# A DeltaNet and SwiGLU kernel: where the heads of the first diagonals lie, and the order of six small steps at its start and end

## The chip, the core and the metric

The kernel runs on one core of a Trainium2 chip. The metric is the device time of one execution in microseconds, the median of several runs.

## The reference

The inputs are q, k, v of shape (4, 8, 768, 48), beta of shape (4, 8, 768), and three weight matrices. The first half is a linear attention with the delta rule, a recurrence over 768 steps for each of the 32 pairs of batch and head:

```python
k_n = k / (norm(k) + 1e-6)
for t in range(S):
    y[:, :, t] = einsum('bhd,bhde->bhe', q[:, :, t], state)
    v_old = einsum('bhde,bhd->bhe', state, k_n[:, :, t])
    state += beta[:, :, t] * einsum('bhd,bhe->bhde', k_n[:, :, t], v[:, :, t] - v_old)
```

The heads of y are then put side by side, x has 3072 rows of 384, and the second half is a feed-forward block with d_ff = 1536:

```python
g = x @ w_gate
out = (g / (1 + exp(-g)) * (x @ w_val)) @ w_out
```

## The kernel before, in words

The sequence is cut into 12 chunks of 64 steps. Within a chunk the recurrence becomes matrix products: the Gram matrix of k with itself (below its diagonal) and with q, the inverse of a triangular matrix, and products with the state. The inverse is found by substitution in blocks of 32 (`R`). A chunk's state is carried to the next by `advance`, which also makes x for that chunk; then the feed-forward block of that chunk runs on TensorE (`gate_val`, `output`; from chunk 2 on `gate_val_fast`, `output_fast`, which save products). The attention part of the next chunks is woven in between by `point`, `fill` and the like. The weights are brought in 42 pieces (`stage`, L262, a load by SyncE; most of the first 18 wait for a piece two or three before them by way of a one-word copy on GpSimd, L261), and each is converted by two passes of ScalarE (`power_step`, L274 and L280) and three of VectorE (`convert`, L293, L301, L313).

The order on each engine is written out by hand: within `manual_schedule` an engine executes its instructions in the order in which the code issues them, and waits in place for its operands. The steps that the change touches lie at the two ends.

The start, in the order of the code from L1929 on:

- `norms(0)` and `norms(1)` square k of the first two chunks on VectorE (L385), add up (L391), and GpSimd takes the root (L395). Between the square and the sums of chunk 0 VectorE clears the last columns of `qpad[0]` (L388).
- SyncE then has q of chunk 0 to load into `qpad[0]` (`load_q(0)`), and behind it on its queue k of chunks 2 and 3, q of chunk 1, v of chunk 0, q of chunk 2 and the first weights. All loads of k, q and v go through `load_heads` (L139) or `load_v` (L185).
- `turned(c, ...)` turns k or q of a chunk on TensorE (L486) and copies it out of PSUM on ScalarE (L488, L490). `first_gram(c)` makes the Gram products of chunk c, 32 of 64x64 (L645; a product of fp32 stands in the profile as two), into two banks of PSUM, one for each parity of the head. Those of chunk 1 go to the banks that the turned k of chunk 1 is copied from.
- `first_diag(c, p)` gathers the two diagonal blocks of 32 by 32 of each head into one tile `flat`, in which the 32 heads of both chunks lie side by side and j, the column, has a stride of 32: one block by ScalarE (L654), the other added by VectorE (L656), once for each parity. `low_copies` puts the blocks below the diagonal into `l_sb` on ScalarE (L669, twelve times).
- VectorE transposes `flat` (L1951), `first_n` and `first_scale` apply norms and beta, and `first_substitution` (L702, L708) inverts both blocks of all heads at once. `first_z` and `spread_z` (L712, L725, L727) put the inverse where TensorE takes it.
- Meanwhile TensorE turns k of chunks 2 and 3 and q of chunks 0 and 1 and makes their Gram products (L502). Where it has nothing to do, `unread` (L638) has it multiply constants into a bank that nobody reads.
- `first_advance` is chunk 0's `advance`: `n_products` (L735) make N, `n_copies` (L741, L749) bring it to SBUF on ScalarE and VectorE; four rounds of products (L954) with copies and sums between (L979, L990, L1002, L1014) give u; then a product with q gives Y (L1022 on), copied at L1029 and L1031, turned for each half `bp` of the batch at L1044 and copied to x at L1045. At L1015, L1032 and L1046 stands an `unread` each.
- Between the steps of `first_advance` the code from L1991 on converts the first weights; `power_step(0)`, ScalarE's two passes over piece 0, stands behind the first step.

The end: `output_fast` of the last chunk stores two tiles `o_sb` with `store` (L1608), each by two DMAs, one for each half of the partitions, all on SyncE's queue (L1610).

Of the kernel before, what the change touches and what calls it, by code (L numbers as in the profile page):

```python
# [14 lines left out]
DP = 64  # L15
R = 32
# [4 lines left out]
def kernel(  # L21
# [25 lines left out]
    nc = tc.nc  # L47

    B, H, S, D = q.shape
    NCH = S // C  # L50
# [7 lines left out]
    HH = NB * H  # L58
# [38 lines left out]
    qpad = [const.tile([128, NB, H, DP], FP32, name=f"qpad{i}") for i in range(QB)]  # L97
# [168 lines left out]
    def power_step(n):  # L266
        if n in powers or n not in staged:
            return
        dst, _, t, f0, m = pieces[n]
        power = words(hp[10 + (n // 2 % 4 if n < N_HALF else (0, 2, 3, 1)[(n + 2) % 4])])  # L270
        power = power[:, n % 2 * m : n % 2 * m + m] if n < N_HALF else power[:, 0:m]
        powers[n] = power
        words_of = staged[n].rearrange("p (f two) -> p f two", two=2)
        nc.scalar.activation(  # L274
            dst[:, t, f0 : f0 + m],
            words_of[:, :, 1].bitcast(FP32),
            ACTF.Copy,
            scale=2.0**-112,
        )
        nc.scalar.activation(power, words_of[:, :, 0], ACTF.Copy, scale=2.0**-29)  # L280
# [100 lines left out]
    def norms(c):  # L381

        ksq = work.tile([128, NB, H, D], FP32, name="ksq", tag="r", bufs=2)
        x = knp[c][:, :, :, 0:D]
        nc.vector.tensor_tensor(out=ksq, in0=x, in1=x, op=ALU.mult)  # L385
        n = n_t[0][:, c].rearrange("p (par bp j) -> p par bp j", par=2, bp=NB)
        if c == 0:
            nc.vector.memset(qpad[0][:, :, :, D - 1 : DP], 0.0)  # L388
        ksq_v = ksq.rearrange("p bp (j par) d -> p par bp j d", par=2)
        for par in range(2):  # L390
            nc.vector.tensor_reduce(  # L391
                out=n[:, par], in_=ksq_v[:, par], axis=mybir.AxisListType.X, op=ALU.add
            )
        n = n_t[0][:, c]
        nc.gpsimd.tensor_tensor(out=n, in0=n, in1=half[:, 0:HH], op=ALU.pow)  # L395
# [58 lines left out]
    def banks(name, tag):  # L454

        if type(tag) is int:
            return [ps_ffn([128, 512], name, tag + i) for i in range(2)]
        p = ps_pair(name, tag)
        return [p[:, 0], p[:, 1]]
# [142 lines left out]
    first_of, l_sb, n_sb = {}, {}, {}  # L602
# [7 lines left out]
    def first_tiles():  # L610
        a = work.tile([128, C * 2 * HH], FP32, name="a_sb")
        for c in range(2):
            l_sb[c] = a[:, R * R * c : R * R * (c + 1)].rearrange(
                "p (h k) -> p h k", k=C
            )
        first_of["flat"] = new_mb().rearrange("p k i -> p (k i)")
        first_of["diag"] = first_of["flat"].rearrange("p (j h) -> p h j", j=R)
        first_of["zb"] = places["z1"].bitcast(FP32)[:, 4 * H_ - 1056 : 4 * H_]
        first_of["mb"] = places["wo"].bitcast(FP32)[:, 2 * H_ : 2 * H_ + 1056]
        nc.vector.memset(first_of["zb"], 0.0)  # L620
        for c in range(2):
            nc.vector.memset(l_sb[c][:, :, 48:C], 0.0)
        for x, rows in enumerate((slice(16, C), slice(R, C), slice(48, C), slice(0, R))):
            nc.vector.tensor_reduce(
                out=m_two[:, x],
                in_=ident.rearrange("p (b n) -> p b n", b=2)[:, :, rows],
                axis=mybir.AxisListType.X,
                op=ALU.add,
            )
        nc.vector.tensor_tensor(  # L630
            out=m_rows, in0=m_two[:, :, 0], in1=m_two[:, :, 1], op=ALU.add
        )
        nc.vector.tensor_scalar_mul(m_low, m_rows[:, 0:3], -1.0)

    def unread(count, p, m=512):

        for _ in range(count):
            nc.tensor.matmul(p[0:R, 0:m], half, half[:, 0:1].to_broadcast([128, m]))  # L638

    def first_gram(c, tag):  # L640

        p_v = [p.rearrange("p (x h i) -> p x h i", x=2, i=R) for p in banks("p_g", tag)]
        for bp, j, par, b, _ in every():
            k_v = kt[c][half_of(par), bp, j, b].rearrange("p (x i) -> p x i", x=2)
            nc.tensor.matmul(  # L645
                p_v[par][half_of(b), :, NJ * bp + j], kt[c][half_of(par), bp, j, b], k_v
            )
        return p_v

    def first_diag(c, p):  # L650
        to = first_of["diag"][:, HH * c : HH * c + HH]
        to = to.rearrange("p (par h) j -> p par h j", par=2)
        for par in range(2):
            nc.scalar.mul(to[:, par], p[par][:, 0], m_rows[:, 3:4])  # L654
        for par in range(2):
            nc.vector.scalar_tensor_tensor(  # L656
                out=to[:, par],
                in0=p[par][:, 1],
                scalar=m_rows[:, 1:2],
                in1=to[:, par],  # L660
                op0=ALU.mult,
                op1=ALU.add,
            )
# [278 lines left out]
    def first_advance():  # L942
# [5 lines left out]
        to = nc.vector.tensor_copy  # L948
# [57 lines left out]
        for bp in range(NB):  # L1006
# [5 lines left out]
                lambda par, b, j: t[there(par, b), 1 - par, bp, j],  # L1012
            )
            plus(uu[:, :, bp], t[:, 1:3, bp], pairs[bp])  # L1014
        unread(1, banks("p_t", 0)[1], 256)  # L1015
        spread_z(1, 0, nc.vector)
        held_loads[26] = lambda: load_v(2)
        yield
# [2 lines left out]
        for bp, copy in enumerate((nc.scalar.copy, nc.vector.tensor_copy)):  # L1021
# [7 lines left out]
            copy(y[:, bp, :, 0], pairs[bp][:, 0])  # L1029
            for b in range(2):  # L1030
                copy(y[half_of(b), bp, :, 1], pairs[bp][half_of(1 - b), 1])  # L1031
        unread(1, banks("p_t", 0)[1], 256)  # L1032
        yield
        y_f = y.rearrange("p bp j par d -> p bp (j par d)")
        xts[0] = x_first
# [5 lines left out]
        for bp, copy in enumerate((nc.scalar.copy, nc.vector.tensor_copy)):  # L1041
            for k in range(KT):
                at = slice(k * 128, (k + 1) * 128)
                nc.tensor.transpose(p_f[bp][:, k], y_f[:, bp, at], ident)  # L1044
            copy(x_v[:, :, bp], p_f[bp])  # L1045
        unread(1, banks("p_t", 0)[1], 256)  # L1046
        spread_z(1, 1, nc.scalar)
        yield
# [558 lines left out]

    def store(c, bp, o_sb):  # L1608
        for b in range(2):
            nc.sync.dma_start(  # L1610
                out=out_v[NB * b + bp, c * C : (c + 1) * C],
                in_=o_sb[half_of(b)],
            )
# [172 lines left out]
    def step(kind, fn, *args):  # L1786
        key = (kind, args or (1,))
        if key not in gens:
            gens[key] = [fn(*args), 0]
        if next(gens[key][0], None) != MORE:  # L1790
            gens[key][1] += 1
# [128 lines left out]
    with tc.manual_schedule(  # L1920
# [8 lines left out]
        new_n(0)  # L1929
        load_beta()  # L1930
        first_tiles()
        norms(0)
        norms(1)
        load_q(0)
# [5 lines left out]
        unread(3, ps_pair("p_t", "px")[:, 0])  # L1940
        turned(0, False, 0)
        p_g = [first_gram(0, "px")]
        first_diag(0, p_g[0])
        turned(1, False, 2)
        p_g.append(first_gram(1, 2))
        first_diag(1, p_g[1])
        spread_beta(copy_a)
# [41 lines left out]
        new_nt(0, spare_of_q, state_flat[:, LEAD : LEAD + 512])  # L1989
        new_nt(1, zb_1.rearrange("p k i -> p (k i)"), spare_of_q[:, 0:512])  # L1990
        gens["advance", (0,)] = [first_advance(), 0]  # L1991
        step("advance", advance, 0)
        power_step(0)
        step("advance", advance, 0)
        converts_first(0)
        power_step(2)
# [110 lines left out]
```

## Time and profile before

| | us |
|---|---|
| median of 3 runs | 663.73 |
| lowest and highest | 663.14, 665.0 |
| the profiled execution | 662.01 |
| its span, first to last instruction | 660.3 |
| TensorE busy in the span | 647.3 |
| VectorE, ScalarE, GpSimd busy | 476.7, 281.5, 198.5 |

The span is what the profile can see; the execution's own time is 1.7 us longer. The mean granted clock of TensorE is 0.997 of full speed. In the rows of a timeline the first two numbers are the start in microseconds from the span's start and the duration; merged instructions have their count behind an x; in brackets stands the idle time of the engine ahead of the row and what ended it. PE is TensorE, PEld its weight loads, ACT ScalarE, DVE VectorE, POOL GpSimd, and SPq SyncE's queue. In a row of a view by stages stand the stretch and its length, each engine's busy time with its count, TensorE's granted clock, the DMA engines' mean share and GB/s.

### The profile page before, as it was taken

To read this page: it belongs to the slowest core of one execution; us is meant where nothing else is said; L and a number is where in the kernel's file an instruction comes from. 1 tells how busy PE (TensorE), PEld (TensorE's weight loads), DVE (VectorE), ACT (ScalarE), POOL (GpSimd) and SP (SyncE) were. 2 spreads that over 40 slices of the span, in tenths; PEclk is the share of its full clock that TensorE was granted. 3 is DMA by queue.
4 is the path that set the end of the run, shared out by engine and by line. 5 is a ranking of instruction groups with operands and counts; after the bars stand their busy time and mean duration, and the time that the engine had idled before them with its cause. 6 is when DMAs were issued, how large, how long until landed. Compare 5 with 4: busy or idle time off the path is not lost.

```text
span 660.3 us, 24914 instructions
## 1 busy us (share of the span) xinstructions
PE 647.3 (98%) x10856; PEld 595.8 (90%) x10856; DVE 476.7 (72%) x991; ACT 281.5 (43%) x626; POOL 198.5 (30%) x310
## 2 busy tenths in 40 slices
PE   8899999999999999999999999999999999999997
PEld 4568888767999999999999999999999999999997
DVE  6879799999688767758667758677758655655562
ACT  5788867124336433434433433532333433334230
POOL 7130041023894032880031881031881000000000
PEclk9999999999999999999999999999999999999999
DMA  9668762005742551373454274363363442222321
GB/s 135 142 173 272 205 164 101 1 14 99 195 81 69 103 117 51 93 140 84 104 127 88 61 164 92 85 135 98 72 136 85 100 105 66 62 94 66 87 66 25
DMA packets 147438, 68.57 MB, mean 104 GB/s; under 512 B 123456, under 2 KB 126560, under 8 KB 147328
## 3 DMA queue, kind: packets, MB, share of 16 engines
q1 hardware_dynamic: 144992, 66.48, 42.6%
q8 instruction: 85, 1.39, 0.8%
q10 hardware_dynamic: 2080, 0.39, 0.4%
q0 software_dynamic: 256, 0.10, 0.1%
q14 instruction: 25, 0.20, 0.1%
HBM read 59.08 MB, written 7.86 MB: 101 GB/s over the span
## 4 chain that ended last, share of the span: by engine, by line
PE 85%; DVE 6%; DMA 4%; SPq 2%; issue 1%; ACT 1%; POOL 0%; DVEq 0%; ACTq 0%; POOLq 0%
PE ffn L1407 40%; PE ffn L1683 21%; PE ffn L1564 8%; DMA h_f<-in_moe_w_val_dram 3%; PE ffn L1593 2%; PE p_px L1169 2%; SPq L139 2%; PE p_py L502 1%; DVE x_t L587 1%; DVE zb L593 1%; PE p_py L1071 1%; PE p_px L1152 1%; PE p_py L1088 1%; PE p_px L502 1%; PE p_px L923 1%
## 5 line engine op out<-in xcount | busy, mean ns | idle before, releaser
L1407 PE MATMUL ffn<-x_t,w_gv 128*128 128x128 f32 x800 | 108.7, 279 | 0.8 <-DVE p_sb L1633 0.7
L1407 PEld LDWEIGHTS ffn<-x_t,w_gv 128*128 128x128 f32 x800 | 97.4, 192 | 3.9 <-DVE p_sb L1633 1.8
L1441 ACT ACTIVATE sil<-ffn 128x256 f32<-128x256 f32 x100 | 36.4, 383 | 115.4 <-PE ffn L1407 109.3
L1407 PE MATMUL ffn<-x_ffn,w_gv 128*128 128x128 f32 x640 | 84.6, 275 | 0.0
L1683 PE MATMUL ffn<-wo_sb,h_f 128*128 128x192 f32 x480 | 83.9, 328 | 0.0
L1683 PEld LDWEIGHTS ffn<-wo_sb,h_f 128*128 128x128 f32 x480 | 77.9, 190 | 0.6
L1407 PEld LDWEIGHTS ffn<-x_ffn,w_gv 128*128 128x128 f32 x640 | 78.0, 192 | 0.3
L822 POOL TENSOR_TENSOR n_b<-mb,half 128x32 f32<-128x32 f32 x5 | 27.6, 5520 | 159.2 <-DVE mb L556 159.2
L587 POOL TENSOR_TENSOR h_f<-zb,mb 128x31 f32<-128x31 f32 (+15 forms) x124 | 69.3, 559 | 19.2 <-PE p_py L800 6.0
L593 POOL TENSOR_TENSOR zb<-zb,h_f 128x31 f32<-128x31 f32 (+15 forms) x124 | 70.6, 569 | 9.7
L1407 PE MATMUL ffn<-x_t,h_f 128*128 128x128 f32 x472 | 64.7, 280 | 0.0
L1407 PEld LDWEIGHTS ffn<-x_t,h_f 128*128 128x128 f32 x472 | 57.3, 192 | 1.6 <-DVE ffn L1633 0.5
L1442 DVE TENSOR_TENSOR h_f<-sil,ffn 128x256 f32<-128x256 f32 x100 | 39.3, 418 | 23.8 <-ACT sil L1441 23.8
L1103 ACT COPY x_ffn<-p_py 32x256 f32<-32x256 f32 (+3 forms) x108 | 39.3, 364 | 29.0 <-PE p_py L1088 27.3
L1633 DVE TENSOR_TENSOR ffn<-p_sb,ffn 128x512 f32<-128x512 f32 x40 | 27.8, 695 | 25.8 <-PE ffn L1407 25.1
L1636 DVE TENSOR_TENSOR ffn<-ffn,p_sb 128x512 f32<-128x512 f32 x40 | 27.5, 691 | 19.9 <-PE ffn L1407 19.1
L1683 PE MATMUL ffn<-last_k,h_f 128*128 128x192 f32 x200 | 36.0, 327 | 0.0
L1636 DVE TENSOR_TENSOR o_sb<-o_sb,ffn 128x192 f32<-128x192 f32 x50 | 17.5, 350 | 24.2 <-PE ffn L1683 23.7
L1564 PE MATMUL ffn<-x_t,w_gv 128*128 128x256 f32 x144 | 33.9, 385 | 0.2 <-DVE x_t L1045 0.2
L1683 PEld LDWEIGHTS ffn<-last_k,h_f 128*128 128x128 f32 x200 | 32.9, 190 | 0.1
L1564 PE MATMUL ffn<-x_ffn,w_gv 128*128 128x256 f32 x144 | 31.9, 380 | 0.0
L1407 PE MATMUL ffn<-x_ffn,h_f 128*128 128x128 f32 x232 | 30.9, 276 | 0.0
(330 smaller groups left out, 1172.7 us busy)
## 6 DMA issues: line engine op xcount, KB each, us to landing
h_f<-w_s SPq DMA_DIRECT2D x81, 256.0 KB, 2.8
more_w<-w_s SPq DMA_DIRECT2D x27, 256.0 KB, 2.8
vin<-in_v_dram SPq DMA_DIRECT2D x48, 96.0 KB, 3.5
out_dram<-o_sb SPq DMA_DIRECT2D x48, 96.0 KB, 2.2
kn<-in_k_dram SPq DMA_DIRECT2D x20, 192.0 KB, 4.7
zt<-in_moe_w_out_dram SPq DMA_DIRECT2D x10, 384.0 KB, 4.3
qpad<-in_q_dram SPq DMA_DIRECT2D x36, 64.0 KB, 3.0
w_s<-h_f SPq DMA_DIRECT2D x7, 256.0 KB, 2.8
```

Source lines behind the costliest of these rows:

```text
L139: dmas[b % len(dmas)].dma_start(out=t[64 * b : 64 * b + 64, :, :, 0:D].rearrange("p bp h d -> p (bp h) d"), in_=halves(x, c, b).rearrange( ...
L587: engine.tensor_tensor(out=t_v, in0=zb[:, 0 : j + 1, j : j + 1].to_broadcast([128, j + 1, m]), in1=mb[:, j : j + 1, j + 1 : R].to_broadcas ...
L593: engine.tensor_tensor(out=zb[:, 0 : j + 1, j + 1 : R], in0=zb[:, 0 : j + 1, j + 1 : R], in1=t_v, op=ALU.add,)
L822: nc.gpsimd.tensor_tensor(out=n, in0=mb.rearrange("p j i -> p (j i)")[:, 0 : R * R : R + 1], in1=half, op=ALU.pow,)
L1103: nc.scalar.copy(x_all[at % 128 : at % 128 + rows, at // 128].rearrange("p (bp b i) -> p bp b i", bp=NB, b=2), p[64 * half + lo : 64 * hal ...
L1407: nc.tensor.matmul(p[:, u], w(u), moving, start=start and u == 0, stop=True, skip_group_check=True,)
L1441: nc.scalar.activation(silu_of, p[:, 0:2], ACTF.Silu)
L1442: nc.vector.tensor_tensor(out=h_of(c, PAIRS[r][e % 3], e // 3), in0=silu_of, in1=p[:, 2:4], op=ALU.mult)
L1564: nc.tensor.matmul(ps[name][:, i], w_sb[:, t, (f + i) * 128 : (f + i + 1) * 128], xts[c][:, t], start=(t == 0 and i == 0), stop=(t == KT - 1),
L1633: nc.vector.tensor_tensor(out=out, in0=a, in1=b, op=ALU.subtract)
L1636: nc.vector.tensor_tensor(out=out, in0=a, in1=b, op=ALU.add)
L1683: nc.tensor.matmul(p[x, part], a(f - f % 2)[:, f % 2], b(f), start=not begun and f == 0, stop=f == FH - 1, skip_group_check=True,)
```

## The change

Six edits:

1. The clearing of `qpad[0]`'s last columns goes from within `norms(0)` to the line ahead of it.
2. In `first_gram` the heads become the innermost dimension of a bank: a product's 64 columns are written at a step of 8 words. `first_diag` then goes over the same order in both places, eight heads side by side, where it read 32 neighbours and wrote them at a stride of 32 words. `low_copies` is not changed, but its reads from PSUM now have a step of 8 words.
3. `first_diag(0)` takes a function to call between its two passes on ScalarE; it is called with the turning of k of chunk 1, whose copies so stand between those passes. TensorE's order stays.
4. `power_step(0)` goes ahead of the first step of `first_advance`, so ScalarE's passes over piece 0 stand ahead of its copy of N.
5. Of the `unread` products in `first_advance`, those ahead of Y's products and behind them are dropped, and one is added between the turnings of the two halves of Y.
6. In the last chunk one of the two DMAs of each `store` is issued by ScalarE in place of SyncE.

```diff
-        if c == 0:
-            nc.vector.memset(qpad[0][:, :, :, D - 1 : DP], 0.0)
...
-        first_of["diag"] = first_of["flat"].rearrange("p (j h) -> p h j", j=R)
...
-        p_v = [p.rearrange("p (x h i) -> p x h i", x=2, i=R) for p in banks("p_g", tag)]
+        p_v = [p.rearrange("p (x i h) -> p x h i", x=2, i=R) for p in banks("p_g", tag)]
...
-    def first_diag(c, p):
-        to = first_of["diag"][:, HH * c : HH * c + HH]
-        to = to.rearrange("p (par h) j -> p par h j", par=2)
+    def first_diag(c, p, between=None):
+        to = first_of["flat"].rearrange("p (j c par h) -> p c par j h", c=2, par=2, j=R)
+        to = to[:, c]
+        p = [p_h.rearrange("p x h j -> p x j h") for p_h in p]
         for par in range(2):
             nc.scalar.mul(to[:, par], p[par][:, 0], m_rows[:, 3:4])
+            if between and par == 0:
+                between()
...
             plus(uu[:, :, bp], t[:, 1:3, bp], pairs[bp])
-        unread(1, banks("p_t", 0)[1], 256)
         spread_z(1, 0, nc.vector)
...
                 copy(y[half_of(b), bp, :, 1], pairs[bp][half_of(1 - b), 1])
-        unread(1, banks("p_t", 0)[1], 256)
         yield
...
             copy(x_v[:, :, bp], p_f[bp])
+            if bp == 0:
+                unread(1, banks("p_t", 0)[1], 256)
         unread(1, banks("p_t", 0)[1], 256)
...
-            nc.sync.dma_start(
+            queue = nc.scalar if c == NCH - 1 and b == bp else nc.sync
+            queue.dma_start(
...
         first_tiles()
+        nc.vector.memset(qpad[0][:, :, :, D - 1 : DP], 0.0)
         norms(0)
...
-        first_diag(0, p_g[0])
-        turned(1, False, 2)
+        first_diag(0, p_g[0], lambda: turned(1, False, 2))
...
+        power_step(0)
         step("advance", advance, 0)
-        power_step(0)
         step("advance", advance, 0)
```

## The prediction

> **What bounds the kernel now.** First the page: its first line says whose time it is.
>
> ```profile
> PE 647.3 (98%) x10856; PEld 595.8 (90%) x10856; DVE 476.7 (72%) x991; ACT 281.5 (43%) x626; POOL 198.5 (30%) x310
> ...
> q8 instruction: 85, 1.39, 0.8%
> ```
>
> TensorE idles 13 of 660.3 us. In a kernel so full, an edit pays where TensorE still waits: the first 48 us and the last 4, where all six edits lie. The span is 660.3 us and the profiled execution 662.01, so 1.7 us lie around the span; the median of the three runs, 663.73, is 1.7 above that execution. The sum is made against 662.01.
>
> Next the chain of waits over the first 70 us (start, us, what):
>
> ```profile
> 0.82 4.71 DMA kn<-in_k_dram
> ...
> 6.60 0.30 DVE qpad L388
> ...
> 6.91 0.60 SPq L139
> ...
> 21.94 1.39 SPq L262
> ...
> 42.00 4.12 DMA h_f<-in_moe_w_val_dram
> ...
> 48.30 1.15 PE p_px L1152 x64
> ```
>
> From 48.30 on it is nearly all TensorE. Ahead of that it is SyncE's row of loads, begun behind the memset of L388, and then weights landing. Beside this runs a second chain of nearly equal length, read from the timelines of single engines: k turned, Gram products, diagonals, substitution, N, x. ScalarE and VectorE there:
>
> ```profile
> 8.52 1.17 ACT L654 ACTIVATE mb<-p_px,m_rows 128x256 f32<-128x256 f32 x2 [0.82 <-issue]
> 9.49 1.11 ACT L488 COPY kt<-ffn 128x512 f32<-128x512 f32 x2
> 11.85 1.17 ACT L654 ACTIVATE mb<-ffn,m_rows 128x256 f32<-128x256 f32 x2 [1.25 <-PE ffn L645]
> ...
> 14.25 1.67 ACT L669 ACTIVATE a_sb<-p_px,m_low 128x128 f32<-128x128 f32 x6
> ...
> 17.25 1.18 ACT L490 COPY kt<-p_py 128x512 f32<-128x512 f32 x2
> ...
> 27.27 0.75 ACT L725 ACTIVATE zt<-mb,m_rows 128x256 f32<-128x256 f32 x1 [2.58 <-DVE mb L712]
> ...
> 33.43 0.48 ACT L990 COPY uu<-p_px 128x384 f32<-128x384 f32 x1 [0.98 <-PE p_px L954]
> ...
> 46.14 0.44 ACT L274 ACTIVATE w_gv<-h_f 128x256 f32<-128x256 f32 x1 [0.49 <-DMA h_f<-in_moe_w_val_dram]
> ...
> 47.47 0.79 ACT L1050 COPY state<-p_px 128x768 f32<-128x768 f32 x1
> ...
> 12.59 1.32 DVE L656 SCALAR_TENSOR_TENSOR mb<-ffn,m_rows,mb 128x256 f32<-128x256 f32 x2 [1.08 <-ACT mb L654]
> 13.95 1.25 DVE L1951 STREAM_TRANSPOSE wo_sb<-mb 128x1024 f32<-128x1024 f32 x1
> ...
> 7.90 5.81 POOL L395 TENSOR_TENSOR n_t<-n_t,half 128x16 f32<-128x16 f32 x2 [0.35 <-DVE n_t L391]
> ```
>
> and TensorE:
>
> ```profile
> 10.65 1.16 PE L645 MATMUL ffn<-kt 64*64 64x64 f32 x62 [0.16 <-ACT kt L488]
> ...
> 23.79 3.63 PE L638 MATMUL ffn<-half 128*32 128x512 f32 x8
> ...
> 28.08 1.16 PE L735 MATMUL ffn<-zt,a_sb 64*64 64x64 f32 x64 [0.66 <-ACT zt L725]
> ...
> 32.63 0.73 PE L954 MATMUL p_px<-v,qpad 64*64 64x48 f32 x22 [1.62 <-issue]
> ...
> 36.63 0.51 PE L954 MATMUL p_px<-x_t,qpad 64*64 64x48 f32 x21 [0.32 <-issue]
> ...
> 39.45 0.62 PE L638 MATMUL ffn<-half 128*32 128x256 f32 x2
> ...
> 40.13 1.17 PE L1044 MATMUL ffn<-ident,y 128*128 128x128 f32 x6
> 40.76 0.31 PEld L1044 LDWEIGHTS ffn<-ident,y 128*128 128x128 f32 x3 [0.32 <-DVE y L1031]
> ...
> 41.24 0.62 PE L638 MATMUL ffn<-half 128*32 128x256 f32 x2
> ```
>
> The two stalls marked "issue" wait for no data. Between 32.63 and 36.63 lie 24 + 32 + 64 + 8 = 128 products. The page has 85 instruction packets of 1.39 MB, 16 KB each; 21,712 products and weight loads in 1.39 MB are 64 bytes apiece, so a packet holds 128 product-and-load pairs. I read the stalls as TensorE waiting for its next block of code, asked for when the block before the last is left: about 4.0 us from one block's entry to the next (32.63 to 36.63), 4.5 the time before (28.08 to 32.63). If so, N's start at 28.08 sets 32.63 and 36.63, and whatever ScalarE does between is covered.
>
> **The change part by part.**
>
> *Memset of qpad ahead of norms(0).* The first load of q (and all of SyncE's row behind it) waits for it:
>
> ```profile
> 3.31 0.17 DVE L633 TENSOR_SCALAR m_low<-m_rows 128x3 f32<-128x3 f32 x1
> ...
> SPq L139 <- DVE qpad L388: 4.4, 1, 4.4
> ...
> 7.00:8.00 1.00, 0.76 (x48) 0.73 (x50) 0.75 (x2) 0.71 (x2) 0.65 (x3) 1.00 0.33 46
> ...
> 14.00:15.00 1.00, 0.67 (x2) 0.00 (x0) 1.00 (x1) 1.00 (x4) 0.00 (x0) 1.00 1.53 160
> ```
>
> Second row: SyncE idles 4.4 us for L388. VectorE is free from 3.5 us (first row), so q is issued near 3.8 instead of 6.91. The transfers cannot gain all 3.1 us: those of k fill the engines first. What goes is the hole behind them, in which 46 GB/s flow (third row, last column) against the 160 of a full microsecond (fourth): 0.7 us, and with its edges about 0.95. Bounds 0.7 and 3.1; I take 1.1, near the hole, because the stretch around 14 us is full in any case. SyncE's DMAs keep their order, so k(2), v and all weights come earlier by this. The early q shares the engines with k(1)'s end; only norms(1) waits for k(1) alone, and it delays L656 of chunk 1 only when it comes more than about 0.9 us later.
>
> *Diagonals side by side.* The four L654 and four L656 lose their stride of 32 words in SBUF. Rows by form:
>
> ```profile
> L654 ACT ACTIVATE mb<-ffn,m_rows 128x256 f32<-128x256 f32 x2 | 1.2, 694 | 1.2 <-PE ffn L645 1.2
> L656 DVE SCALAR_TENSOR_TENSOR mb<-ffn,m_rows,mb 128x256 f32<-128x256 f32 x2 | 1.3, 706 | 1.1 <-ACT mb L654 1.1
> L274 ACT ACTIVATE w_gv<-h_f 128x256 f32<-128x256 f32 x2 | 0.9, 434 | 0.0
> L301 DVE SCALAR_TENSOR_TENSOR w_gv<-w_gv,h_f 128x256 uint32<-128x256 uint32 x10 | 4.0, 420 | 0.2
> ```
>
> Equal sizes without the stride (last two rows) take 434 and 420 ns, against 694 and 706. From chunk 1's Gram to the transpose stand one L654 and two L656: 2.10 us (11.85 to 13.95) becomes some 1.3. Gain 0.8 on VectorE's chain. In exchange 64 Gram products write PSUM at a step of 8 words and twelve L669 read it so. No row has a PSUM step. Bounds (no gain: nothing there has a stride to lose): L669 as now (1.67 us for six), or as much more as L725, which reads SBUF at a stride, has over L274 (0.75 - 0.43 us for 256 elements, 0.16 for 128): 0 to 1.9 us for twelve; a Gram 1.16 us as now, or double. I take nothing: a product of 512 columns takes 0.45 us (3.63 / 8 at 23.79), a pace at which a step need not show; both ends stay.
>
> *Turned k(1) between the two ScalarE passes.* The copies (L488) start when their four transposes are done, about 9.0 (the first L654, now 0.43, is over by then), not 9.49: the second Gram, which waits for both copies since it writes their banks (row at 10.65), ends 0.48 earlier. ScalarE's second L654 comes after them, at about 10.1, and its reader on VectorE is still through before chunk 1's.
>
> So VectorE's chain comes 0.48 + 0.8 = 1.28 earlier at L1951, which then ends at 13.9. The norms follow it, and GpSimd's two powers end at 13.7 (7.90 + 5.81; 0.2 sooner without the memset), so they still do not come last. The substitution keeps its length, and L725 at 27.27 becomes 26.0. ScalarE's row (L669, k(2), k(3), q copies) and TensorE's unread products come 0.48 earlier: they end at 26.95 instead of 27.43 (23.79 + 3.63). N starts at the later of 26.95 and 26.75 (26.0 and L725's 0.75): 26.95 instead of 28.08. **Gain 1.1 us**, now set by TensorE's own unread products.
>
> *Piece 0's passes ahead of N's copies.* 0.75 us of ScalarE (L274, L280) move from 31.70 to about 27.7. Queued behind them are N's copy (0.25 later than the shift) and v's copies; the products after them stop at the code stall in any case. At the old place ScalarE waited 0.98 (row at 33.43). So nothing either way: the stall covers it; with the cover gone, 0.3 lost and up to 0.5 gained.
>
> *Unread products.* The one before Y and the one after it go: TensorE then waits where it multiplied (about 0.7 and 0.6 us). The new one, two passes (0.62 in all, 0.4 of it passing), sits ahead of the second turnings, which now begin at 40.76 and would wait for it until about 40.9: 0.1 on x, less than the unread product ahead of the first gate that x waits beside. I take nothing; bounds -0.1 and 0.2.
>
> *State and weights.* The state copy at 47.47 follows ScalarE's passes, which waited 0.49 for a weight. With both chains 1.1 earlier, L1152 starts at about 47.2. Everything behind keeps its distances. Sum so far: -1.1.
>
> *Last stores.*
>
> ```profile
> 656.16 0.35 DVE L1636 TENSOR_TENSOR o_sb<-o_sb,ffn 128x192 f32<-128x192 f32 x1 [1.60 <-PE ffn L1683]
> 656.60 1.11 SPq L1610 DMA_DIRECT2D out_dram<-o_sb  x2
> ```
>
> Two issues of 0.55 in a row become one on each queue; ScalarE has nothing left. At most 0.55 goes, less if the two transfers then slow each other: I take 0.45.
>
> Total: -1.1 - 0.45 = **-1.55**: 660.5 for an execution like the profiled one, 662.2 against the median.
>
> The Trainium skill speaks against the diagonals: PSUM — Partial Sum Buffer, Specifications, has PSUM lines of 8 bytes and says that any non-contiguous pattern slows matmuls significantly. No row here shows it; by that rule the steps cost, and the time is that of the third rival below.
>
> **The rivals.**
>
> *More than that.* TensorE's code stall of 1.62 us shrinks because the block's fetch meets a quieter queue, or SyncE's 3.1 us count more fully. For it: with 4.0 instead of 4.5 us per block, 0.5; with the stall gone, another 0.5. Then -1.1 - 1.0 - 0.45 = -2.55: **661.2**. Against it: weight loads are in flight in both kernels.
>
> *Only the tail.* The weights land as late as now (42.00 in the chain, and 46.14 on ScalarE), since each load waits for the one two before it, and the state copy stays at 47.47; the change then does not do what it says at the start. For it: the wait of 0.49. Against: their first issue, at 21.94, stands in SyncE's row. -0.45: **663.3**.
>
> *Slower: steps in PSUM.* Place: the 64 Gram products and twelve L669. Grams double: second Gram's end 1.2 later instead of 0.48 earlier; L669 adds 1.9; TensorE's unread products end at 27.43 + 3.1 = 30.5, N starts 2.4 later; less the tail 0.45: +2.0, **665.7**. It decides from 0.48 + 0.65 (N's present wait behind the unread products) + 0.45 = 1.6 us on that row of ScalarE. For it: every strided SBUF row above is slower by 0.26 to 0.32. Against: fp32 products pass slowly.
>
> *The clock.* After the stall of 1.62 the granted clock fell by half:
>
> ```profile
> 33.00:34.00 1.00, 1.00 (x48) 1.00 (x44) 0.97 (x2) 0.48 (x1) 0.98 (x2) 0.50 0.21 78
> ```
>
> With two unread products gone, gaps of 0.7 and 0.6 us could call a second such stretch, near 40 us: some 0.7 us of its products, so -0.85, **662.9**. The microseconds around 14.67 to 15.78 idled 1.1 without it (clock 1.00 in the row at 14), so I hold it unlikely. The Trainium skill, TensorE: Matmul & The Clock Gate, "HAM oscillation", wants idle of a window of about 3.4 us before the clock falls; the trace shows it after less, so that sentence is no comfort here.
>
> **How the numbers follow.** Forecast 662.2: 42 in 100, spread about 0.8 either way by what the clock does. More, 661.2: 25. Only the tail, or the clock: 18 together. Steps: 15, of which half is one of the two costs alone (about 664) and half the whole, 665.7 and above. 0.3% (2.0 us) is about what a measurement of this kernel can tell from no change: faster is below 661.74, slower above 665.72. Faster: nearly all of the second and 4 in 10 of the first, 0.42. Slower: 0.09. Within: 0.49. The range from 660.4 to 665.0 leaves out about 1 in 10 at either end.
>
> **What would show it.** Right: SyncE's q issue near 3.8; L654 and L656 near 0.43 in mean; L735 at about 27.0; L1152 at about 47.2; stores landing 0.45 earlier behind the last VectorE add. Wrong: L645 or L669 longer than now; L735 later than 28.08; the 128-pair stalls not moving with L735; a second 0.50 in the clock; or a time that moves without L1152.

## The result and the profile after

The kernel after takes 662.66 us in the median of 20 executions (659.75 to 665.33), the kernel before 664.94 in 20 executions beside it (663.04 to 669.79). The ratio is 0.9967 with a 95% interval from 0.9954 to 0.9981: 2.2 us faster, between 1.3 and 3.1. The forecast was 1.55 us.

The profiled execution of the kernel after took 662.8 us, with a span of 661.1; that of before, on which the prediction's sum stands, took 662.01, which is below the lowest of the 20 executions measured beside the kernel after. So the two traces can't be subtracted as wholes; stage by stage they can. The page's first line, after:

```profile
PE 647.7 (98%) x10854; PEld 595.2 (90%) x10854; DVE 476.4 (72%) x991; ACT 281.0 (43%) x626; POOL 198.6 (30%) x310
```

TensorE has two passes less (one fp32 product of `unread`) and idles 13.4 of 661.1 us, against 13.0 of 660.3. Next VectorE's timeline of the kernel after at the start:

```profile
3.48 0.28 DVE L1933 MEMSET qpad<- 128x272 f32 x1
...
10.56 0.88 DVE L656 SCALAR_TENSOR_TENSOR mb<-p_px,m_rows,mb 128x256 f32<-128x256 f32 x2 [0.21 <-ACT mb L652]
11.91 0.88 DVE L656 SCALAR_TENSOR_TENSOR mb<-ffn,m_rows,mb 128x256 f32<-128x256 f32 x2 [0.47 <-ACT mb L652]
12.82 1.25 DVE L1952 STREAM_TRANSPOSE wo_sb<-mb 128x1024 f32<-128x1024 f32 x1
```

The clearing is done at 3.8, the pairs of L656 take 0.88 us instead of 1.32, and the transpose begins at 12.82 instead of 13.95. ScalarE (L652 is the former L654):

```profile
8.53 0.47 ACT L652 ACTIVATE mb<-p_px,m_rows 128x256 f32<-128x256 f32 x1 [0.82 <-PE p_px L642]
9.08 1.07 ACT L486 COPY kt<-ffn 128x512 f32<-128x512 f32 x2
10.04 0.49 ACT L652 ACTIVATE mb<-p_px,m_rows 128x256 f32<-128x256 f32 x1
11.41 0.84 ACT L652 ACTIVATE mb<-ffn,m_rows 128x256 f32<-128x256 f32 x2 [0.88 <-PE ffn L642]
13.31 0.32 ACT L430 COPY beta_b<-p_py 128x192 f32<-128x192 f32 x1 [1.07 <-PE p_py L423]
13.90 1.07 ACT L486 COPY qt<-ffn 128x512 f32<-128x512 f32 x2 [0.27 <-PE ffn L484]
14.86 1.67 ACT L669 ACTIVATE a_sb<-p_px,m_low 128x128 f32<-128x128 f32 x6
16.36 1.71 ACT L669 ACTIVATE a_sb<-ffn,m_low 128x128 f32<-128x128 f32 x6
...
26.15 0.75 ACT L725 ACTIVATE zt<-mb,m_rows 128x256 f32<-128x256 f32 x1 [0.85 <-DVE mb L712]
...
45.35 0.44 ACT L274 ACTIVATE w_gv<-wo_sb 128x256 f32<-128x256 f32 x1 [0.88 <-DMA wo_sb<-in_moe_w_gate_dram]
...
46.03 0.78 ACT L1050 COPY state<-p_px 128x768 f32<-128x768 f32 x1
```

Up to 12 us the row is as forecast. Then ScalarE waits 1.07 us for L423, the spreading of beta on TensorE, and the six L669, forecast 0.48 earlier than 14.25, stand at 14.86. TensorE:

```profile
10.21 1.16 PE L642 MATMUL ffn<-kt 64*64 64x64 f32 x62 [0.16 <-ACT kt L486]
...
12.43 0.85 PE L423 MATMUL p_py<-wo_sb,ident 16*32 16x192 f32 x8 [0.29 <-DMA wo_sb<-in_beta_dram]
...
24.40 3.63 PE L635 MATMUL ffn<-half 128*32 128x512 f32 x8
27.96 1.16 PE L735 MATMUL ffn<-zt,a_sb 64*64 64x64 f32 x64
...
30.24 0.76 PE L954 MATMUL p_px<-v,qpad 64*64 64x48 f32 x29 [0.19 <-ACT v L979]
...
34.49 0.51 PE L954 MATMUL p_px<-x_t,qpad 64*64 64x48 f32 x21 [0.62 <-issue]
...
45.16 0.35 PE L735 MATMUL ffn<-zt,a_sb 64*64 64x64 f32 x9 [0.62 <-issue]
...
46.93 1.15 PE L1152 MATMUL p_px<-state,kt 48*64 48x48 f32 x64
...
56.55 0.72 PE L1196 MATMUL p_px<-v,zb 64*64 64x48 f32 x33 [1.58 <-issue]
```

N starts at 27.96, only 0.12 us earlier than before. L1152 starts at 46.93 instead of 48.30, since the "issue" stall of 1.62 us in the n-times-v products is not there (30.24). But a stall of 1.58 us now stands at 56.55, where this execution loses all of that again. What holds the start is seen in the chain of waits of the kernel after, and in the issues of beta's loads in the first 14 us (KB each, median us from issue to landing), first before, then after:

```profile
7.03 5.26 DMA wo_sb<-in_beta_dram
12.43 0.85 PE p_py L423 x8
...
14.97 3.10 ACT a_sb L669 x12
...
24.47 2.90 PE ffn L635 x7
```

```profile
wo_sb<-in_beta_dram POOLq DMA_DIRECT2D x4, 20.0 KB, 2.9
wo_sb<-in_beta_dram POOLq DMA_DIRECT2D x4, 4.0 KB, 3.2
```

```profile
wo_sb<-in_beta_dram POOLq DMA_DIRECT2D x4, 20.0 KB, 5.1
wo_sb<-in_beta_dram POOLq DMA_DIRECT2D x4, 4.0 KB, 5.6
```

The early load of q shares the DMA engines with beta's eight small loads, which GpSimd issues from 2.7 to 7.5 us in both kernels. In these two executions they take 2.2 to 2.4 us longer, TensorE waits for them at L423, and ScalarE and TensorE's row to N behind it.

The end, after:

```profile
657.19 0.35 DVE L1637 TENSOR_TENSOR o_sb<-o_sb,ffn 128x192 f32<-128x192 f32 x1 [1.59 <-PE ffn L1684]
657.62 0.53 ACTq L1611 DMA_DIRECT2D out_dram<-o_sb  x1
657.64 0.47 SPq L1611 DMA_DIRECT2D out_dram<-o_sb  x1
```

The last tile's two stores are issued side by side. From the end of the last add (657.54) to the end of the span (661.06) it is 3.52 us; before it was 3.79.

### The profile page after: what moved, and what is told of

Same layout as the page of the kernel before. It is cut to its first block, busy times and chain, and to the rows that moved or that the text cites. A ratio compares the mean times of both kernels' runs of the same rounds, so it can differ in the third digit from the quotient of the medians.

```text
span 661.1 us, 24911 instructions
## 1 busy us (share of the span) xinstructions
PE 647.7 (98%) x10854; PEld 595.2 (90%) x10854; DVE 476.4 (72%) x991; ACT 281.0 (43%) x626; POOL 198.6 (30%) x310
## 4 chain that ended last, share of the span: by engine, by line
PE 82%; DVE 8%; ACT 4%; DMA 3%; issue 2%; POOL 1%; DVEq 0%; ACTq 0%; SPq 0%; POOLq 0%
PE ffn L1407 40%; PE ffn L1684 21%; PE ffn L1564 4%; PE ffn L1593 2%; DMA zt<-in_moe_w_out_dram 2%; PE p_px L1169 2%; DVE x_t L585 1%; DVE zb L591 1%; PE p_px L500 1%; PE p_py L500 1%; PE p_py L1071 1%; PE p_px L923 1%; PE p_py L1088 1%; PE p_px L1152 1%; DMA wo_sb<-in_beta_dram 1%
## 5 line engine op out<-in xcount | busy, mean ns | idle before, releaser
L822 POOL TENSOR_TENSOR n_b<-mb,half 128x32 f32<-128x32 f32 x5 | 27.6, 5520 | 160.9 <-DVE mb L554 160.9
```

Source lines behind the costliest of these rows:

```text
L822: nc.gpsimd.tensor_tensor(out=n, in0=mb.rearrange("p j i -> p (j i)")[:, 0 : R * R : R + 1], in1=half, op=ALU.pow,)
```

## The experiments

The theory behind the first runs (A): the gain comes from VectorE's chain, the diagonals; the early clearing costs through beta; the stalls marked "issue" are TensorE's waits for code. The first rival: the gain comes from SyncE's earlier row. All medians stand beside the kernel before on the same chip; "us against before" is the ratio's interval times its median there (664.2 to 664.8). Each run's profile is of one execution; those of e7 and e8 are the longest of their twelve. A pair number counts TensorE's product-and-load pairs from the start of the program; by the prediction's reading a block of code holds 128 of them, and a border is where one block ends.

| run | edits of the change | median | us against before |
|---|---|---|---|
| e1 | 1 | 663.93 | -0.9 (-1.9 to +0.1) |
| e2 | 2, 3 | 661.25 | -3.3 (-4.6 to -2.1) |
| e3 | 6 | 663.71 | -0.3 (-1.6 to +1.0) |
| e4 | all but 1 | 662.17 | -2.1 (-3.3 to -0.9) |
| e5 | 4, 5 | 663.37 | -1.1 (-2.4 to +0.1) |
| e6 | all, 24 more pairs ahead of N | 665.12 | +1.1 (-0.5 to +2.7) |
| e7 | all, beta spread later | 662.29 | -2.2 (-3.5 to -0.8) |
| e8 | all, both of these | 664.24 | -0.4 (-1.7 to +0.9) |
| e9 | 2, 3, 6 | 661.75 | -2.9 (-3.8 to -1.9) |
| e10 | 2, 3, 6, two more unread | 662.02 | -2.9 (-4.1 to -1.8) |
| e11 | 1, 2, 3, 6, beta later, two more unread | 662.08 | -2.4 (-3.5 to -1.3) |
| e12 | all, beta later, two more unread | 662.42 | -2.0 (-3.5 to -0.5) |

**e1, the early clearing alone.**

```diff
-        if c == 0:
-            nc.vector.memset(qpad[0][:, :, :, D - 1 : DP], 0.0)
...
+        nc.vector.memset(qpad[0][:, :, :, D - 1 : DP], 0.0)
         norms(0)
```

> The kernel before with edit 1 alone (the clearing of qpad[0] ahead of norms(0)). Theory A (beta's collision): q's early transfer takes DMA time from beta's eight small loads on GpSimd's queue, which land near 12.3 us instead of about 10; TensorE waits for beta at L425 until about 12.4, ScalarE's row from L488 (copies of the turned q) on is 0.4 to 0.7 us later than before, N's start (first L735 row) is at 28.1 to 28.7 us, not earlier, and the median lies within 0.5 us of before, although the first weight pieces land 0.8 us earlier. Theory B (my forecast's step): SyncE's whole row comes 1.1 us earlier, ScalarE's row does not come later, and L1152 starts some 0.5 to 1 us earlier: about -0.8 us.

Beta's loads took 5.2 and 5.6 us, N started at 28.75 us, L1152 at 49.91, and the median is 0.9 us below before, with an interval that just includes nothing. A is right on beta's loads, but not on the median, which fits B; B's earlier L1152 isn't in this trace, that of the second longest of twelve executions. On N the run decides nothing. The first diagonal pass came 0.68 us late by itself (9.20), so that beta was there at L423, and N starts as far behind that pass as before: 19.55 us, against 19.56.

**e2, the diagonals alone.**

```diff
...
-        p_v = [p.rearrange("p (x h i) -> p x h i", x=2, i=R) for p in banks("p_g", tag)]
+        p_v = [p.rearrange("p (x i h) -> p x h i", x=2, i=R) for p in banks("p_g", tag)]
...
-        first_diag(0, p_g[0])
-        turned(1, False, 2)
+        first_diag(0, p_g[0], lambda: turned(1, False, 2))
```

> The kernel before with edits 2 and 3 alone (heads side by side in the diagonals, the copies of k(1) between the two passes). Theory A: VectorE's chain is 1.1 to 1.3 us earlier (L725 on ScalarE at about 26.1 instead of 27.27), and, as beta is not delayed here, ScalarE's row and TensorE's unread products are 0.4 to 0.5 us earlier too, so N starts at 26.9 to 27.1 instead of 28.08. The weights stay where they were, so that L1152 gains less than N: -0.3 to -1.0 us in the median. Theory B (the gain of the whole change comes from SyncE's row): N starts earlier but the median stays within 0.3 us of before. Theory C (a step in PSUM costs): L645 or L669 longer than the 1.16 and 1.67 us of before by 0.2 or more.

The largest gain of any single part, more than A expected: 3.3 us. The Gram took 1.15 us and six L669 1.68: C (a step in PSUM) falls. N started at 27.45, 0.5 later than expected, because this execution's first diagonal pass was 0.5 us late (9.03). Behind that pass N comes 18.42 us later, 1.14 less than before.

**e3, the two queues alone.**

```diff
+            queue = nc.scalar if c == NCH - 1 and b == bp else nc.sync
-            nc.sync.dma_start(
+            queue.dma_start(
```

> The kernel before with edit 6 alone (one of each two last stores issued by ScalarE). Theory A (issue is serial on one queue): the last transfer is issued 0.55 us earlier, the span behind the last VectorE add shrinks by 0.2 to 0.55 us, median -0.2 to -0.55. Theory B (most of the 2.3 us of the whole change comes from the tail): -1 us or more.

From the last add's end to the span's end: 3.53 us here, 3.52 in the kernel after, 3.55 in e4 and 3.53 in e9; without the edit 3.79 before, 3.78 in e1, 3.88 in e2. So 0.2 to 0.4 us in each pair of traces, which a median can't resolve. B falls.

**e4, everything but the early clearing.**

```diff
+        if c == 0:
+            nc.vector.memset(qpad[0][:, :, :, D - 1 : DP], 0.0)
...
-        nc.vector.memset(qpad[0][:, :, :, D - 1 : DP], 0.0)
         norms(0)
```

> The kernel after with edit 1 undone (the clearing back within norms(0)). Theory A: without q's early transfer beta lands near 10 us as in the kernel before, ScalarE's row is about 1 us earlier than in the kernel after (first L669 row at 13.8 instead of 14.86), N starts at 26.9 to 27.1 instead of 27.96; but the weights land 0.8 to 1.5 us later than in the kernel after, so L1152 starts at about 47.3 to 47.8. Median -1.0 to -2.0 us against before, about that of the kernel after. Theory B (SyncE's row carries the gain): L1152 back near 48.3 and the median within 0.7 us of before.

Beta's loads took 3.7 and 4.4 us, the first L669 stood at 14.19, N at 27.30 and L1152 at 47.91. The median is that of the kernel after (-2.1 against -2.2): no gain from the early clearing shows in this company, with intervals of about 1 us either way, and B falls. N's start 0.66 us earlier does not show in the median either.

**e5, the pass over piece 0 and the unread products alone.**

```diff
+        power_step(0)
         step("advance", advance, 0)
-        power_step(0)
         step("advance", advance, 0)
...
-        unread(1, banks("p_t", 0)[1], 256)
         spread_z(1, 0, nc.vector)
...
-        unread(1, banks("p_t", 0)[1], 256)
         yield
         y_f = y.rearrange("p bp j par d -> p bp (j par d)")
...
             copy(x_v[:, :, bp], p_f[bp])
+            if bp == 0:
+                unread(1, banks("p_t", 0)[1], 256)
```

> The kernel before with edits 4 and 5 alone (ScalarE's passes over piece 0 ahead of N's copies; the unread products of first_advance). Theory A: nothing at the start moves, N starts at 28.1 us as before, what is saved or lost between N and Y lies beside TensorE's waits for code; median within 0.6 us of before. Theory B: the gaps left by the dropped unread products lower the granted clock more often than before (mean clock of the executions below before's by 0.002 or more), +0.7 to +1.7 us. Theory C: these two edits carry part of the gain, -0.7 us or more.

N started at 28.36 us and L1152 at 49.68. The median is 1.1 us below before with an interval from -2.4 to +0.1: not told apart from nothing. A loss of more than 0.1 us is excluded; whether they gain is not settled, for A's and C's medians both lie in the interval. B falls: the mean clock is 0.9962, and 0.9959 before.

**e6, 24 more pairs of code ahead of N.**

```diff
-        unread(4, banks("p_t", 2)[0])
+        unread(16, banks("p_t", 2)[0], 128)
```

> The kernel after, in which the four unread products of 512 columns ahead of N are sixteen of 128 columns: the same columns, 24 more product-and-load pairs ahead of N, nothing else. Theory A (TensorE's issue stalls are waits for a block of 128 pairs of code): the stalls stay at the pairs with the numbers 600, 728, 984 and 1240, which are now products that stand 24 earlier in the kernel's order, and the border at pair 472 is crossed among the unread products, near 26 us, instead of just behind N's start at 28; so the next blocks come up to 2 us earlier and the stalls between N and Y together are 0.5 to 1.5 us shorter; median 0.3 to 1.5 us below the kernel after, -2.5 to -3.7 against before. Theory B (the stalls wait for data or for another engine): they stay at the same products of the kernel's order, whose pair numbers are then 624, 752, 1008; the median stays at that of the kernel after.

TensorE's timeline in e6:

```profile
23.76 2.07 PE L635 MATMUL ffn<-half 128*32 128x128 f32 x17
27.07 1.82 PE L635 MATMUL ffn<-half 128*32 128x128 f32 x15 [1.24 <-issue]
28.82 1.16 PE L735 MATMUL ffn<-zt,a_sb 64*64 64x64 f32 x64
...
31.06 0.39 PE L954 MATMUL p_py<-vin,zt 64*64 64x48 f32 x13 [0.39 <-issue]
```

On the place A is right: the stall that stood 8 products deep in the n-times-v products stands 24 earlier in the order, at pair 600 again, and pair 728 has its stall again (0.67 us, at 34.79). On the time: a stall of 1.24 us opens in the middle of the unread row, at pair 473. The 16 KB that landed last ahead of it were on their way from 24.21 to 25.79; in the kernel after they were in at 25.26, and their border was reached only at N's start. N starts 0.86 later than in the kernel after. And yet this is not where the run loses: counted product by product, TensorE is 0.8 us ahead of the kernel after from 60 us on, as A has it, because the stall of 1.58 at 56.55 is gone. It falls behind at 534 us, where a second new stall opens:

```profile
535.89 0.82 PE L1407 MATMUL ffn<-x_t,w_gv 128*128 128x128 f32 x5 [1.64 <-issue]
```

It stands three products behind the 128 small ones of L905, and 16 KB of code landed 1.37 us ahead of its end, as at the stalls near the start. Among the other runs only e8 has it. So the 24 pairs moved the borders of the whole program, and a late one came to lie badly. The median is 2.5 us above the kernel after, and A is wrong on it. This trace is of one of the six shorter executions (662.66 to 664.30); the six longer ones (665.94 to 668.15, mean clock 0.986 to 0.994) left none, so why they are longer stays open.

**e7, beta spread behind q's turning.**

```diff
-        spread_beta(copy_a)
         turned(0, True, 0)
+        spread_beta(copy_a)
```

> The kernel after with spread_beta behind the turning of q of chunk 0 instead of ahead of it. Theory A (beta's late landing holds TensorE and, through it, ScalarE's row): the copies of the turned q start at about 12.6 instead of 13.90, the first L669 at 13.6 to 14.2 instead of 14.86, N starts at 26.9 to 27.2 instead of 27.96, then set by L725 on ScalarE (26.15 + 0.75); 0.3 to 1.0 us below the kernel after. Theory B (N's start is held by something else on ScalarE or TensorE): N's start stays at 27.7 or later and the median within 0.3 us of the kernel after.

ScalarE and TensorE in e7:

```profile
13.86 1.66 ACT L669 ACTIVATE a_sb<-p_px,m_low 128x128 f32<-128x128 f32 x6
```

```profile
27.15 1.16 PE L735 MATMUL ffn<-zt,a_sb 64*64 64x64 f32 x64
...
32.20 0.51 PE L954 MATMUL p_px<-v,qpad 64*64 64x48 f32 x21 [2.12 <-issue]
```

Beta's loads still took 5.2 and 5.6 us, but nothing waited for them: the first L669 came 1.0 us and N 0.81 us earlier than in the kernel after, as A has it. The median did not follow (-2.2 both). The last row shows a reason in this execution, the longest of twelve: the earlier N ran into a longer wait for code.

**e8, both.** The two diffs of e6 and e7 together.

> The kernel after with both of the two other edits of this call: spread_beta behind q's turning, and sixteen unread products of 128 columns in place of four of 512. Theory A: both gains, N's start at about 27 and the border at pair 472 crossed near 25; 0.8 to 2.3 us below the kernel after, -3 to -4.5 against before. Theory B: once the next block of code sets the pace between N and Y, an earlier start of N is covered, and the two together bring no more than the shift alone.

2.0 us above e7, as e6 is 2.5 above the kernel after: the cost of the shifted code borders repeats, and both theories of this run were too hopeful. The late stall is at the same product:

```profile
538.58 1.27 PE L1407 MATMUL ffn<-x_t,w_gv 128*128 128x128 f32 x5 [1.69 <-issue]
```

Behind it, from 538.79, lie 3.41 us at half clock. Up to 527 us this trace is 1.4 us ahead of e7's, from 540 us on 2.2 behind.

**e9, the diagonals and the tail.** The diffs of e2 and e3 together.

> The kernel before with edits 2, 3 and 6 alone (diagonals side by side, the copies of k(1) between, the two queues of the last stores): the change without the early clearing, the early pass over piece 0 and the moves of unread products. Theory A (the diagonals carry the gain, the early clearing gives part of it back through beta): N starts at 27.2 to 27.6 us, at the same granted clock 2.4 to 3.4 us below before, so -2.3 to -3.7 in the median. Theory B (the low median of the run with the diagonals alone was chance): -0.7 to -1.6, no more than the whole change.

ScalarE, then TensorE, in e9:

```profile
13.77 1.67 ACT L671 ACTIVATE a_sb<-p_px,m_low 128x128 f32<-128x128 f32 x6
```

```profile
23.32 3.63 PE L637 MATMUL ffn<-half 128*32 128x512 f32 x8
26.91 1.16 PE L737 MATMUL ffn<-zt,a_sb 64*64 64x64 f32 x64
...
31.02 0.51 PE L956 MATMUL p_px<-v,qpad 64*64 64x48 f32 x21 [1.19 <-issue]
```

This is the start that the prediction worked out: L669 0.48 earlier than before, N at 26.91 (26.95 forecast), still set by the unread row. The median is 2.9 us below before: A, though N comes earlier than the 27.2 to 27.6 that A gave.

Ahead of e10 the price that its expectation puts on the clock: of the 25 executions of before beside e1 to e4, five with a mean clock of 0.997 took 663.27 us in mean, three with 0.991 665.42 (but five with 1.000 took 663.84). Over all kernels to e9 it is some 3.5 us for 0.01 of clock, or 0.9 for 3.41 us at half, which are 0.0026 of the span.

**e10, two unread products more.** The diff is against e9.

```diff
         yield MORE
+        unread(1, banks("p_t", 0)[1], 512)
         for bp in range(NB):
...
         yield MORE
+        unread(1, banks("p_t", 0)[1], 256)
         for bp in range(NB):
```

> The kernel before with edits 2, 3 and 6, and two more unread products on TensorE: one of 512 columns ahead of the products of N with v, one of 256 columns ahead of those of N with t, both just ahead of a border of code where TensorE waits. Theory A (the half clock follows a stretch in which TensorE is busy less than about 0.6 of the time, and each stretch of 3.41 us costs about 0.9 us): the waits are filled, the half-clock stretches between 32 and 44 us become fewer, the mean clock of the executions rises by 0.002 or more over the kernel without the two products, and the median falls by 0.5 to 1 us under it. Theory B (the clock does not follow TensorE's busy share, or the added 1.35 us of products stand on the path): the clock stays and the median rises by 0.3 to 1.3 us.

The mean clock rose to 0.9998 over its six executions, from 0.9982 over nine in e9, and the median did not move (-2.9 both): filled waits bring a fuller clock, as A says, and the price that A puts on it doesn't show. With intervals of about 1 us either way and 1.35 us of added products a gain of half a microsecond isn't excluded. That executions at a lower clock are longer may come from longer waits, which bring both; this is argued, not shown.

**e11 and e12, beta later and two unread products more, without and with edits 4 and 5.** The diffs of e7 and e10 on top of edits 1, 2, 3 and 6, and of the whole change.

> The kernel of the run with the two more unread products, with edit 1 besides (the early clearing) and spread_beta behind the turning of q, which takes beta's late landing off TensorE's row. Theory A (the early weights are worth something once beta holds nothing): N starts at 26.9 to 27.3, ScalarE waits for no weight at 46 us, L1152 0.5 us or more earlier; 0.3 to 1 us below the run without these two. Theory B (from N to the first gates the pace is set by code and clock): no difference over 0.4 us.

> The kernel after, all six edits in it, with spread_beta behind the turning of q and the two more unread products (512 columns ahead of the products of N with v, 256 ahead of those of N with t). Theory A (what the kernel after loses is beta's late landing, about 0.9 us at the same clock, and half-clock stretches, about 1.3 us at its mean clock of 0.9963): mean clock 0.998 or more, N's start at 26.9 to 27.4, median 0.5 to 1.5 us under the kernel after's 662.66, that is 661.2 to 662.2, or -2.4 to -3.6 against before. Theory B (filled waits and an earlier N are given back to waits for code after 48 us, as the runs without edits 4 and 5 let one think): no difference from the kernel after over 0.5 us, -1.7 to -2.7 against before.

Mean clocks 0.9992 and 0.9989, N at 27.23 and 27.46; against before 0.5 and 0.9 us less is gained than in e9, with intervals that overlap. B in both: e11 stands 0.06 us above e10, and e12 brings nothing over the kernel after that the measurement can tell. The stretch from 30 to 40 us in the profiled executions of e9, e12 and e10 (length, then each engine's busy time, then the granted clock):

```profile
30.00:40.00 10.00, 8.21 (x253) 6.32 (x253) 6.66 (x14) 6.63 (x18) 3.81 (x7) 0.66 0.61 163
```

```profile
30.00:40.00 10.00, 7.41 (x265) 5.05 (x263) 5.98 (x15) 7.00 (x19) 2.94 (x5) 1.00 0.53 128
```

```profile
30.00:40.00 10.00, 8.10 (x271) 5.49 (x270) 7.35 (x16) 7.38 (x20) 3.58 (x6) 1.00 0.70 179
```

The mean clock of these 10 us is 0.66 in e9 and 1.00 in e12, and yet from N's start to L1152 it takes 20.74 us in e9 (26.91 to 47.65) and 20.82 in e12 (27.46 to 48.28), which has 1.35 us more of unread products and edits 4 and 5. The nearer neighbour of e9 is e10, which has the two products alone: 19.79 us (27.02 to 46.81) at a clock of 1.00. By 113 us its lead over e9 is gone. So what half the clock costs here is not settled; in the medians no cost shows.

## Why the prediction was right, and where it was not

The time was right and the direction too: -1.55 forecast, -2.2 measured, with -1.55 inside the interval. The steps did not all hold:

*Diagonals side by side, and k(1) turned between.* Right in mechanism and nearly in size. L652 and L656 take 0.47 to 0.49 and 0.48 us (two of L656 in a row 0.88) instead of the 434 and 420 ns of the rows borrowed; from chunk 1's Gram to the transpose it is 1.41 us (11.41 to 12.82), where 1.3 was forecast and 2.10 stood before; the second Gram ends 0.44 earlier, 0.48 forecast; VectorE's chain gains 1.13 instead of 1.28. e9 shows the start that this was to give, to 0.04 us.

*A step in PSUM.* Taken at nothing, and it is nothing: the Gram 1.16 us before and after, six L669 1.67 and 1.67. The page PSUM — Partial Sum Buffer (Specifications) of the Trainium skill, by which non-contiguous patterns slow matmuls significantly, does not hold for these fp32 products of 64 columns. The slower rival's steps are there and their price is zero.

*N's start.* This step failed. "26.95 instead of 28.08" became 27.96. The prediction let the early q share the engines "with k(1)'s end" and asked who waits for k(1); it did not ask which other loads are in flight. GpSimd's eight loads of beta are, and TensorE's L423 stands ahead of q's turning. In the kernel after the first L669 comes 6.33 us behind the first diagonal pass, in e4, e9 and e7 5.33, 5.27 and 5.37: the early clearing costs 1.0 us there, by way of beta. N starts 19.56 us behind that pass in before, 18.41 to 18.44 in e2, e4 and e9, 19.43 in the kernel after and 18.42 in e12, which has the early clearing but spreads beta later. In e6's execution, with beta's loads at 4.8 and 5.2 us, the cost to L669 is 0.3.

*The memset's 1.1 us on the weights.* SyncE's q issue stands at 3.79, as forecast. The first weight is issued at 21.09 instead of 21.94, 0.85 earlier; but at 21.14 in e9 and 21.18 in e3, which have no early clearing. And by e4 it was worth nothing that can be told from the medians.

*L1152 at about 47.2.* It came at 46.93, for another reason than forecast: not N's earlier start but the missing 1.62 us stall. That is the "more" rival's first mechanism, and the rival was given 25 in 100. It was this execution's luck: the 16 KB for pair 600 set out as pair 472 was entered (28.13), where before it was 2.11 us later and in the twelve runs 0.7 to 3.5.

*"Everything behind keeps its distances."* Wrong. From L1152 to the last add it is 607.86 us in the trace of before and 610.26 in that of after, 608.02 to 609.29 in e1 to e4. Counted product by product, after is 1.38 us ahead of before at L1152, 0.45 behind from 60 us on, 0.79 from 113 and 1.03 from 540; in between the two run in parallel. The waits for code move: the one at pair 600 (8 products into n times v) takes 1.62 before, nothing after, 1.28 in e2, 2.12 in e7; the one at pair 1240 nothing before, 1.58 after, 0.74 in e4, 1.29 in e7.

*Waits for code.* The reading was right: in e6 the stalls kept their pair numbers, not their products. In the fourteen traces there are 40 stalls of over 0.3 us marked "issue" behind 22 us, and each ends 1.2 to 1.6 us after 16 KB of TensorE's code have landed. In the trace of before the 16 KB that belong to pair 600 are on their way from 30.36 to 31.32, and TensorE goes on at 32.63. From N's start to the end of that stall it is 3.5 to 5.1 us in before, e1, e2, e3, e4, e7 and e9, against the 4.0 to 4.5 forecast. So an earlier N does make the next stall end earlier, in part; but with executions of one kernel 2 to 7 us apart, single ones don't show it. The Trainium skill, Runtime: NRT & Kernel Launch, Instruction fetch mechanics, calls the crossing of a 16 KB block mostly hidden; these rows show up to 2.1 us of TensorE in the open.

*Piece 0's passes.* Right: they stand at 27.74 to 28.51, ahead of N's copies at 29.22, and nothing waits for them. *Unread products:* nothing that e5 could tell.

*The tail.* Right in mechanism, mis-sized: 0.27 us instead of 0.45. The last two issues stand side by side (657.62, 657.64) and end 0.6 us behind the last add, where it was 1.2 before. About 0.3 of that is lost again behind them: a store on ScalarE's queue takes 2.4 us to land, on SyncE's 2.1 before and after.

*The clock.* No second stretch came in the profiled execution; the one at 32.84 moved to 36.26. A cost doesn't show: e10 to e12 have nearly full clock and no better median, as far as intervals of 1 us or more can tell.

So the sum was near in part by luck: its terms are partly wrong. The diagonals are worth 3.3 us alone and 2.9 with the tail (e2, e9), twice what their rows explain (1.17 us at N in e9 and 0.27 at the tail), and the whole change, which contains them, 2.2, though N gains only 0.12 in its trace. The intervals of e2, e9 and the kernel after overlap, so that the other edits cost something is not shown; that they add anything isn't either. Where the second half of the diagonals' gain arises stays open: the traces point at the waits for code between 28 and 57 us, which differ from execution to execution; no run here held them still.

Best of all versions measured are e2 and e9, without edits 1, 4 and 5. They beat the kernel before surely, the kernel after only by medians of different series (-3.3 and -2.9 against -2.2, each beside before).

## What to carry to other kernels

Moving a transfer forward moves it into someone else's time: list every load in flight there, small ones on other queues too, and who stands behind them in order. If one profiled execution lies outside the range of the timed ones, use its rows for stages and not for the end. Where many small products run, the next block of code may set the pace; then an earlier start upstream, a fuller clock and a filled gap may bring nothing that can be measured, and a few more instructions can cost more than they do as work, even far behind the place where they were put (24 pairs at 26 us opened a stall at 534 us).

## What the runs showed of the hardware

- TensorE's half clock comes in stretches of 3.41 us or of two, three and four times that: 3.41 in before, after, e2, e3 and e6, 6.83 in e1, e4, e5 and e9, 10.24 in e8 (and 3.41 more at 539 us), 13.65 in e7, none ahead of the last stores in e10, e11 and e12. In the 3.41 us ahead of each of the first ones TensorE was busy 0.34 to 0.59 of the time, never idle throughout. The row of the kernel after for 37 to 39 us has the clock behind the busy times:

```profile
37.00:39.00 2.00, 1.79 (x27) 1.10 (x21) 1.07 (x3) 1.74 (x6) 0.00 (x0) 0.50 0.76 214
```

- TensorE waits in the open for its code: 40 stalls of 0.3 to 2.1 us in fourteen traces end 1.2 to 1.6 us after the landing of 16 KB, and up to pair 1496 they lie multiples of 128 product-and-load pairs apart, to within one.
- 24 pairs more, with the same columns in all, cost 2.5 and 2.0 us in the median (e6 against the kernel after, e8 against e7). In both traces borders moved, and a stall of 1.64 and 1.69 us opened at 534 and 537 us.
- Eight loads of 20 and 4 KB on GpSimd's queue took 4.8 to 5.3 and 5.2 to 5.8 us to land (medians of seven traces) beside SyncE's early load of q, and 2.9 to 3.9 and 3.2 to 4.5 in the seven traces without it.
